# Attention and two mixtures of experts on one core: two cleared tiles of the router, and where job 14 puts a sum

## The chip, the core and the metric

The kernel runs on one core of a Trainium2 chip. The metric is the device time of one execution in microseconds, as the median of three runs. One execution is profiled, and all rows below are of that one.

## What is computed

Three layers follow each other. The first is attention over 2 batches x 8 heads, where each pair of queries is averaged. Its output becomes 1152 rows of 512. The second layer (called moe1 here) runs every row through 4 experts and adds the results with weights. The third (moe2) sends every row to the one expert of 8 with the highest score.

```python
q_pool = q.reshape(B, H, S // 2, 2, D).mean(axis=3)          # B,H,S,D = 2,8,1152,64
scores = scale * q_pool @ k.transpose(0, 1, 3, 2)
attn = exp(scores - max); attn /= attn.sum(-1) + 1e-9
x = (attn @ v) as [1152, 512]
for e in range(4):  out += p[:, e] * (relu(x @ w1[e]) @ w2[e])
x = out
logits = normalised(x) @ normalised(expert_emb).T / tau       # 8 experts
idx = argmax(logits); gate = softmax(logits)[idx]
for e in range(8):  out[idx == e] = gate * (relu(x[idx == e] @ w1[e]) @ w2[e])
```

## The kernel before

**Attention** is cut into 16 jobs (`g` = 0 to 15). A job is a pair of heads and one part of their queries: 256 columns in an even job, 320 in an odd one. `streams` multiplies keys by queries for nine chunks of 128 keys (L120, into PSUM tiles `S`, two for each of the two heads), and ACT takes the exponential of each into a tile `E` (L123, ten of them). POOL adds the nine `E` of a job into `es` (L148; the tile is shown as `y` in odd jobs). `av` multiplies the `E` by v on PE (L154), two products for each chunk. `total(g)` multiplies `es` by ones on PE (L157), which gives the denominators, and ACT copies them out as `r` (L159). `norm` has three steps: ACT copies the products out of PSUM as `x` (L163), DVE takes the reciprocal of `r` in two halves (L165), and DVE multiplies `x` by it (L167). `normalise(g)` is `total` and the last two steps. `fin` splits the normalised `x` into a high part (ACT, L174) and a low part (POOL, for job 15 DVE, L175), which the first layer of moe1 reads.

The jobs overlap: the sum and the normalising of job 13 stand inside job 14, in the middle of its products with v (L228), those of job 14 stand behind the products of job 15 (L245), and those of job 15 (`end`, L247) stand in moe1 between the first and the second layer of its first batch.

**moe1** takes the rows in three batches of 384 for each of four experts. In the first layer, eight groups of twelve matmuls (L301 to L303) fill one of three PSUM tiles `ps` each; ACT and DVE read a group out as `hh` (L305) and `hl` (L306), after which its tile can be filled again. Weights come by DMA and are split into a high and a low part by ACT (L262) and DVE (L265). The second layer (L316 to L318) follows.

**The router** (`router`, L406) prepares moe2. `block(t)` runs once for each 128 rows when moe1 has finished them, at about 572 us for the first; `place`, `table` and `finish` make the lists of rows. Two of its tiles are cleared by a memset on DVE: the first row of `base` (how many rows each expert has had so far, L416) and the last three columns of `ear` (L494). Both tiles are in a pool that is opened after attention's pools have been closed, so they lie in memory that attention used.

The program's text is not the order of the work. Where `manual_schedule` is on, the order is that of the text for attention, and for moe1's first expert on PE, ACT and DVE; elsewhere a scheduler places each instruction as early as it finds. It put both memsets, which need no input, in the middle of attention's end.

Of the kernel before, what the change touches and what calls it, by code (L numbers as in the profile page):

```python
# [9 lines left out]
def attention(tc, q, k, v, xT, identF, cc, rp, emb, tau, prep, begin, second, keep, NJ=16):  # L10
# [7 lines left out]
    with ExitStack() as ctx:  # L18
# [13 lines left out]
        def load(p):  # L32
            b,h0=divmod(2*p,H)
            kn=ld.tile([128,NC,2,D],F32,name="kn"); qn=ld.tile([128,2,5,2,D],F32,name="qn"); vn=vp.tile([128,2,NC,D],F32,name="vn")
            st['ld',p]=kn,qn; st['v',p]=vn
            ek,eq=(nc.sync,nc.scalar) if p==0 else (nc.sync,nc.sync)
            ks=[slice(0,3),slice(3,6),slice(6,9)] if p==0 else [slice(0,9)]
            for n in range(2):
                eq.dma_start(qn[:,n,0:4],q[b,h0+n,0:1024].rearrange("(i p r) d -> p i r d",p=128,r=2))
                eq.dma_start(qn[:,n,4],q[b,h0+n,896:1152].rearrange("(p r) d -> p r d",r=2))  # L40
            for c in ks:
                for n in range(2): ek.dma_start(kn[:,c,n],k[b,h0+n].rearrange("(p c) d -> p c d",c=NC)[:,c])
            if p>1: load_v(p)
        def load_v(p):
            b,h0=divmod(2*p,H)
            for n in range(2): (nc.scalar if p==0 else nc.sync).dma_start(st['v',p][:,n],v[b,h0+n].rearrange("(p c) d -> p c d",c=NC))
        def qsum(p):
            qn=st['ld',p][1]
            qs=kq.tile([128,5,2,D],F32,name="qs",bufs=1); st['qs',p]=qs
            qv=qn.rearrange("p h i r d -> p i h r d")  # L50
            for n in range(2): (nc.gpsimd if p else nc.vector).tensor_tensor(out=qs[:,:,n],in0=qv[:,:,n,0],in1=qv[:,:,n,1],op=ALU.add)
# [41 lines left out]
        def smax(g,i,early=False):  # L93
            for h in range(2): smax1(g,i,h,early)
# [5 lines left out]
        def neg(g):  # L100

            u=g%2; m=st.pop(('m3',g)); M=MM[u]
            nc.vector.tensor_reduce(out=M[:,0:2,:,0],in_=m[:,0:2],axis=AX.X,op=ALU.max,negate=True)
            if u: nc.vector.tensor_reduce(out=M[:,2,:,0],in_=m[:,2,0:1].to_broadcast([128,2,3]),axis=AX.X,op=ALU.max,negate=True)
# [44 lines left out]
        def av(g,c0,c1):  # L149
            p,u=divmod(g,2); n=JOB[u][1]; vn=st['v',p]  # L150
            if c0==0: st['O',g]=psO.tile([128,320],F32,name="O"); st['x',g]=keep['x'] if g==NG-1 else fp.tile([128,320],F32,name="x")
            O=st['O',g]
            for c in range(c0,c1):
                for h in range(2): nc.tensor.matmul(O[HD[h],0:n],vn[:,h,c],st['E',g,c][:,h,0:n],start=c==0,stop=c==NC-1)  # L154
# [5 lines left out]
        def norm(g,n0):  # L160
            n=JOB[g%2][1]; r=st.get(('r',g)); x=st['x',g]
            if n0==0:
                nc.scalar.copy(x[:,0:n],st['O',g][:,0:n])  # L163
            if n0==1:
                for a in range(0,n,n//2): nc.vector.reciprocal(r[:,a:a+n//2],r[:,a:a+n//2])  # L165
            if n0==2:
                nc.vector.tensor_tensor(out=x[:,0:n],in0=x[:,0:n],in1=r[:,0:n],op=ALU.mult)  # L167
# [10 lines left out]
        def E1(): return ep.tile([128,2,320],F32,name="E").rearrange("p h n -> p (h n)")  # L178
        route_emb_load(nc,cc,E1(),one.tile([128,1],F32,name="tb"),emb,tau)
        with tc.manual_schedule():  # L180
            qsum(0)
            load(1)
            kT(0,0); kT(0,1); st['low',0](); qT(0)
            smax(0,0,True); smax(0,1,True); st['low',1]()
            kT(0,2); st['low',2]()
            norms,scale,turn=route_emb(tc,cc,rp,E1(),one.tile([128,5],F32,name="n2"),identF)
            norms()
            for i in range(2,6): smax(0,i,True)
            scale()
            load_v(0)  # L190
            neg(0); mT(0)
            load_v(1)
            def normalise(g): total(g); norm(g,1); norm(g,2)
            for g in range(NG):
                p,u=divmod(g,2); last=g==NG-1

                rl=[(j,i) for j,i in [(g+1,i) for i in (3,4,5)]+[(g+2,i) for i in (0,1,2)] if j<NG]
                if g==0: qsum(1)
                elif u==0 and p+2<NP: load(p+2)
                elif g==NG-4: begin()  # L200
                elif u and p+2<NP: qsum(p+2)
                def between(c,hh,i):
                    if hh==1 and i==3 and c==2 and last: fin(g-2)
                def whole():

                    if not last: mT(g+1)
                    if u==0 and p+1<NP:
                        for c in range(3): tmax(p+1,c,S1(c,384) if c<2 else None)
                    if u and p+2<NP:
                        for n in range(3): kT(p+2,n,S1(n,384) if n<2 else None)  # L210
                        qT(p+2)
                if g==0:
                    streams(0,range(C1),[(1,i) for i in range(6)],PAT[3],between)
                    for c in range(3): tmax(0,c)
                    turn(T1(32).rearrange("p (d e) -> p d e",e=8))
                    for n in range(3): kT(1,n)
                    neg(1); qT(1)
                    load(2)
                    streams(0,range(C1,NC),rl[3:],PAT[2],between)
                    whole()  # L220
                    av(0,0,NC); norm(0,0)
                elif (1, 1)[u]:
                    streams(g,range(NC),rl,PAT[0],between)
                    whole()
                    if g>1 and not last: fin(g-2)
                    if g==NG-2: prep[0][2]()
                    if not last:
                        av(g,0,2); normalise(g-1)  # L228
                        if g==NG-3:
                            for i in range(3): prep[i][1]()  # L230
                        if g==NG-2: prep[3][1](); prep[1][2]()
                        av(g,2,NC); norm(g,0)
                else:
                    streams(g,range(C1),rl[:3],PAT[1],between)
                    if g>1 and not last: fin(g-2)
                    if not last:
                        normalise(g-1); av(g,0,3)
                    streams(g,range(C1,NC),rl[3:],PAT[2],between)
                    if not last:
                        whole()  # L240
                        av(g,3,NC); norm(g,0)
            g=NG-1
            prep[2][2](); prep[3][2]()
            kqx.close(); second()
            av(g,0,NC); normalise(g-1); norm(g,0); fin(g-1)  # L245
# [160 lines left out]
def router(tc, c, rp, keep, psX, y, ysc, al, identF):  # L406
    nc=tc.nc
    V=nc.vector
# [4 lines left out]
    oh=P('oh',[NT,8],BF16); gate=P('gate',[NT]); base=P('base',[NT+1,8]); R=P('R',[NT])  # L413
    ro=P('ro',[NT]); gp=P('gp',[NT,3],BF16)
    ear=P('ear',[NT]); q=P('q',[NT]); Bm=P('Bm',[NT,128],BF16)
    V.memset(base[:,0],0.0)  # L416
    es=P('es',[2,8]); ei=K('ei',[2],I32)
    cap=P('cap',[8]); sv=P('sv',[8])
    res={'ei':ei}
    def block(t):  # L420
        def S(name,shape): return rp.tile([128]+shape,F32,name="r_"+name,bufs=2)
        ts=slice(t,t+1)
# [14 lines left out]
        rk=psX.tile([128,2,8],F32,name="lr")  # L437
        nc.tensor.matmul(rk[:,1],c['ones'],oh[:,t],start=True,stop=True)
        nc.tensor.matmul(rk[:,0],c['low'],oh[:,t],start=True,stop=True)
        V.tensor_tensor(out=base[:,t+1],in0=base[:,t],in1=rk[:,1],op=ALU.add)  # L440
        rank=S('rank',[8]); V.tensor_tensor(out=rank,in0=rk[:,0],in1=base[:,t],op=ALU.add)
        w=S('w',[8]); V.tensor_tensor(out=w,in0=oh[:,t],in1=rank,op=ALU.mult)
# [41 lines left out]
    def place(a,b):  # L484

        n=b-a; ts=slice(a,b)
        ls=look(f'ls{a}',sv,a,b)
        if a==0:
            lc=look(f'lc{a}',cap,a,b)
            V.tensor_tensor(out=ear[:,ts],in0=R[:,ts],in1=lc,op=ALU.is_lt)  # L490
            ne=P('ne',[n]); V.tensor_scalar(out=ne,in0=ear[:,ts],scalar1=-1.0,scalar2=1.0,op0=ALU.mult,op1=ALU.add)
            l0=ls; ls=P('l0',[n]); V.tensor_tensor(out=ls,in0=l0,in1=ne,op=ALU.mult)
        else:
            V.memset(ear[:,ts],0.0)  # L494
        r2=P(f'r2{a}',[n]); V.tensor_tensor(out=r2,in0=R[:,ts],in1=ls,op=ALU.subtract)
        qm=P(f'qm{a}',[n,9]); V.tensor_tensor(out=qm,in0=bc(r2[:,:,None],[n,9]),in1=bc(c['thr'][:,None,1:10],[n,9]),op=ALU.is_ge)
        V.tensor_reduce(out=q[:,ts],in_=qm,axis=AX.X,op=ALU.add)
        V.scalar_tensor_tensor(out=ro[:,ts],in0=q[:,ts],scalar=-128.0,in1=r2,op0=ALU.mult,op1=ALU.add)

        g=gate[:,ts]  # L500
        V.tensor_copy(gp[:,ts,0],g)
        g1=P(f'g1{a}',[n]); V.tensor_tensor(out=g1,in0=g,in1=gp[:,ts,0],op=ALU.subtract)
        V.tensor_copy(gp[:,ts,1],g1)
        V.tensor_tensor(out=gp[:,ts,2],in0=g1,in1=gp[:,ts,1],op=ALU.subtract)
# [366 lines left out]
```

## Time and profile before

| | |
|---|---|
| median of three runs | 798.37 us (797.63 to 798.45) |
| the profiled execution | 798.72 us, of which the span from first to last instruction is 797.0 us |
| PE (TensorE matmul) busy | 769.5 us, 97% of the span |
| DVE, ACT, POOL busy | 387.0, 316.5 and 252.5 us |
| mean granted clock of TensorE | 0.993 |

Every engine works through its own queue in order; an instruction at its head that waits holds all that stand behind it. In the rows, an idle time stands in brackets behind the instruction that ended it, with what released it; "issue" means that the profile shows no releaser. Durations of successive matmuls overlap, so the step from start to start is what one costs.

### The profile page before, as it was taken

To read this page: it belongs to the slowest core of one execution; us is meant where nothing else is said; L and a number is where in the kernel's file an instruction comes from. 1 tells how busy PE (TensorE), PEld (TensorE's weight loads), DVE (VectorE), ACT (ScalarE), POOL (GpSimd) and SP (SyncE) were. 2 spreads that over 40 slices of the span, in tenths; PEclk is the share of its full clock that TensorE was granted. 3 is DMA by queue.
4 is the path that set the end of the run, shared out by engine and by line. 5 is a ranking of instruction groups with operands and counts; after the bars stand their busy time and mean duration, and the time that the engine had idled before them with its cause. 6 is when DMAs were issued, how large, how long until landed. Compare 5 with 4: busy or idle time off the path is not lost. (4 is left out here: it accounts for less than half of the span.)

```text
span 797.0 us, 13133 instructions
## 1 busy us (share of the span) xinstructions
PE 769.5 (97%) x5112; PEld 648.9 (81%) x5112; DVE 387.0 (49%) x815; ACT 316.5 (40%) x722; POOL 252.5 (32%) x224
## 2 busy tenths in 40 slices
PE   5999999999997999999999999999999999999996
PEld 3787878787767898998989989899898889877773
DVE  4778888888764220251214412144252568574520
ACT  3477667676871121250103301033131354474611
POOL 4489999999996000000000000000000201231001
PEclk9999999999998999999999999999999999999999
DMA  8412332140043100150003100000044141888992
GB/s 225 116 49 46 94 94 66 30 164 2 6 128 137 49 1 1 30 208 0 1 1 107 53 1 1 1 1 0 27 146 185 51 162 31 313 281 312 329 354 89
DMA packets 57735, 77.52 MB, mean 97 GB/s; under 512 B 23031, under 2 KB 33271, under 8 KB 57664
## 3 DMA queue, kind: packets, MB, share of 16 engines
q1 hardware_dynamic: 54272, 70.35, 26.7%
q0 software_dynamic: 1600, 4.98, 1.8%
q10 hardware_dynamic: 1792, 1.26, 0.6%
q8 instruction: 42, 0.69, 0.4%
q14 instruction: 29, 0.24, 0.1%
HBM read 71.86 MB, written 4.98 MB: 96 GB/s over the span
## 5 line engine op out<-in xcount | busy, mean ns | idle before, releaser
L301 PE MATMUL ps<-xb,w 128*128 128x384 f32 x384 | 130.6, 340 | 5.2 <-DVE hl L306 5.2
L303 PE MATMUL ps<-xb,w 128*128 128x384 f32 x384 | 130.3, 339 | 0.0
L447 POOL TENSOR_TENSOR r_n<-r_ss,half 128x1 f32<-128x1 f32 x9 | 5.3, 587 | 392.1 <-ACT X L446 392.1
L305 ACT ACTIVATE hh<-ps 128x384 fp32r<-128x384 f32 x96 | 47.1, 492 | 203.0 <-PE ps L303 203.0
L306 DVE SCALAR_TENSOR_TENSOR hl<-ps,hh 128x384 fp32r<-128x384 f32 x96 | 53.4, 556 | 148.6 <-ACT hh L305 148.4
L318 PE MATMUL py<-w,hl 128*128 128x512 f32 x288 | 113.5, 394 | 0.0
L317 PE MATMUL py<-w,hh 128*128 128x512 f32 x288 | 113.2, 393 | 0.0
L316 PE MATMUL py<-w,hh 128*128 128x512 f32 x288 | 112.8, 392 | 0.0
L123 ACT ACTIVATE E<-S 128x320 f32<-128x320 f32 (+1 forms) x288 | 98.7, 411 | 18.0 <-PE S L120 11.1
L90 DVE TENSOR_REDUCE m<-T 128x1 f32<-128x384 f32 x180 | 89.9, 549 | 18.1 <-PE T L89 16.6
L302 PE MATMUL ps<-xc,w 128*128 128x384 f32 x288 | 97.6, 339 | 0.0
L265 DVE TENSOR_TENSOR w<-st,w 128x1024 fp32r<-128x1024 f32 x60 | 76.0, 1290 | 39.2 <-ACT w L262 38.4
L148 POOL TENSOR_TENSOR y<-y,E 128x640 f32<-128x640 f32 x56 | 89.9, 1605 | 4.3
L120 PE MATMUL S<-qh,kh 64*128 64x320 f32 (+1 forms) x288 | 85.9, 342 | 0.0
L120 PE MATMUL S<-qh,kl 64*128 64x320 f32 (+1 forms) x288 | 80.2, 305 | 0.0
L148 POOL TENSOR_TENSOR es<-es,E 128x512 f32<-128x512 f32 x56 | 75.4, 1347 | 11.5 <-ACT E L123 7.4
L120 PE MATMUL S<-ql,kh 64*128 64x320 f32 (+1 forms) x288 | 78.0, 303 | 0.0
L301 PEld LDWEIGHTS ps<-xb,w 128*128 128x128 f32 x384 | 72.9, 190 | 6.3 <-DVE hl L306 5.5
L120 PE MATMUL S<-mr,ones 64*128 64x320 f32 (+1 forms) x288 | 76.3, 295 | 0.0
L154 PE MATMUL O<-E,vn 128*64 128x320 f32 (+1 forms) x576 | 75.7, 408 | 0.0
L262 ACT CAST w<-st 128x1024 fp32r<-128x1024 f32 x60 | 60.9, 1050 | 33.5 <-PE py L318 22.7
L303 PEld LDWEIGHTS ps<-xb,w 128*128 128x128 f32 x384 | 72.8, 190 | 0.0
(377 smaller groups left out, 1470.1 us busy)
## 6 DMA issues: line engine op xcount, KB each, us to landing
st<-in_moe_w SPq DMA_DIRECT2D x104, 512.0 KB, 6.2
kn<-in_k SPq DMA_DIRECT2D x14, 288.0 KB, 4.8
vn<-in_v SPq DMA_DIRECT2D x14, 288.0 KB, 3.3
qn<-in_q SPq DMA_DIRECT2D x14, 256.0 KB, 4.2
ysc<-y SPq DMA_DIRECT2D x9, 256.0 KB, 2.1
qn<-in_q SPq DMA_DIRECT2D x14, 64.0 KB, 3.5
kn<-in_k SPq DMA_DIRECT2D x6, 96.0 KB, 4.0
vn<-in_v ACTq DMA_DIRECT2D x2, 288.0 KB, 6.1
```

What stands on the lines that cost most here:

```text
L90: nc.vector.tensor_reduce(out=m[:,t,h,c:c+1],in_=s,axis=AX.X,op=ALU.max)
L120: nc.tensor.matmul(s,l[hd],r[hd],start=i==0,stop=i==3)
L123: nc.scalar.activation(out=st['E',g,c][:,h,0:n],in_=s,func=AF.Exp)
L148: nc.gpsimd.tensor_tensor(out=s,in0=st['E',g,0][:,:,0:n] if c==1 else s,in1=st['E',g,c][:,:,0:n],op=ALU.add)
L154: for h in range(2): nc.tensor.matmul(O[HD[h],0:n],vn[:,h,c],st['E',g,c][:,h,0:n],start=c==0,stop=c==NC-1)
L265: def low(): (nc.vector if le=='V' else nc.gpsimd).tensor_tensor(out=wl,in0=st,in1=wh.bitcast(F32),op=ALU.subtract)
L301: nc.tensor.matmul(ps,wh[:,fs],xh[dc],start=(dc==0),stop=False)
L302: nc.tensor.matmul(ps,wh[:,fs],xl[dc],start=False,stop=False)
L303: nc.tensor.matmul(ps,wl[:,fs],xh[dc],start=False,stop=(dc==3))
L316: nc.tensor.matmul(py,hh[:,us],wh[:,cs],start=(fc==0),stop=False)
L317: nc.tensor.matmul(py,hh[:,us],wl[:,cs],start=False,stop=False)
L318: nc.tensor.matmul(py,hl[:,us],wh[:,cs],start=False,stop=(fc==7))
```

## The change

It has two parts. The two memsets are replaced by multiplications by zero, which have to wait for their input: `base` takes its zeros from the first count of rows in block 0, `ear` from the ranks `R` of the last three blocks. And in job 14 alone (`g==NG-2`), all 18 products with v (a matmul for each half of a pair) come first, then the sum of job 13; before, 4 stood ahead of it and 14 behind.

```diff
@@ attention @@
                     if not last:
-                        av(g,0,2); normalise(g-1)
+                        c=NC if g==NG-2 else 2
+                        av(g,0,c); normalise(g-1)
                         if g==NG-3:
                             for i in range(3): prep[i][1]()
                         if g==NG-2: prep[3][1](); prep[1][2]()
-                        av(g,2,NC); norm(g,0)
+                        av(g,c,NC); norm(g,0)
@@ router @@
-    V.memset(base[:,0],0.0)
@@ block @@
         nc.tensor.matmul(rk[:,0],c['low'],oh[:,t],start=True,stop=True)
+        if t==0: V.tensor_scalar(out=base[:,0],in0=rk[:,1],scalar1=0.0,scalar2=None,op0=ALU.mult)
         V.tensor_tensor(out=base[:,t+1],in0=base[:,t],in1=rk[:,1],op=ALU.add)
@@ place @@
-            V.memset(ear[:,ts],0.0)
+            V.tensor_scalar(out=ear[:,ts],in0=R[:,ts],scalar1=0.0,scalar2=None,op0=ALU.mult)
```

What that does to the order of the instructions is seen at three places. In the new kernel the line numbers of code that follows an added line are higher by one or two. The first place is DVE at the end of attention: the last splits of weights, the normalising of job 14 (256 columns), and the first read-outs of moe1. Before:

```order
L265 TENSOR_TENSOR w<-st,w 128x1024 [waits DMAHW1_49,Activation_49]
L265 TENSOR_TENSOR w<-st,w 128x1024 [waits DMAHW2_49,PE_49,Activation_49]
L265 TENSOR_TENSOR w<-st,w 128x1024 [waits DMAHW4_49,PE_49,Activation_49]
L416 MEMSET base 128x8 [waits DMAHW5_49,PE_49]
L494 MEMSET ear 128x3 [waits Pool_49]
L165 RECIPROCAL r<-r 128x128 [waits Activation_49]
L165 RECIPROCAL r<-r 128x128
L167 TENSOR_TENSOR x<-x,r 128x256 [waits DVE_49]
L306 SCALAR_TENSOR_TENSOR hl<-ps,hh 128x384 [waits Activation_49] x2
L265 TENSOR_TENSOR w<-st,w 128x1024 [waits DMAHW5_49]
```

The same place now:

```order
L266 TENSOR_TENSOR w<-st,w 128x1024 [waits DMAHW1_49,Activation_49]
L266 TENSOR_TENSOR w<-st,w 128x1024 [waits DMAHW2_49,PE_49,Activation_49]
L266 TENSOR_TENSOR w<-st,w 128x1024 [waits DMAHW4_49,PE_49,Activation_49]
L165 RECIPROCAL r<-r 128x128 [waits Activation_49]
L165 RECIPROCAL r<-r 128x128
L167 TENSOR_TENSOR x<-x,r 128x256 [waits DVE_49,Pool_49]
L307 SCALAR_TENSOR_TENSOR hl<-ps,hh 128x384 [waits DMAHW5_49,Activation_49] x2
L266 TENSOR_TENSOR w<-st,w 128x1024 [waits DMAHW5_49]
L307 SCALAR_TENSOR_TENSOR hl<-ps,hh 128x384 [waits Activation_49] x2
```

The memsets are gone from here, with their waits for PE, a DMA queue and POOL; the multiplication of `x` has got a wait for POOL of its own, and the read-outs one for the DMA queue. The second place is PE in job 14, around the sum of job 13 (`y_106` by `y_107`), as a difference:

```order
 L120 MATMUL S_3687<-mr_3514,ones 128x256
 L109 MATMUL T<-identF,MM_147 128x128 x3
-L154 MATMUL O<-E,vn 64x256 x4
+L154 MATMUL O<-E,vn 64x256 x18
 L157 MATMUL T<-y_106,y_107 64x320 x2
-L154 MATMUL O<-E,vn 64x256 x14
 L120 MATMUL S_3743<-qh,kh 128x320
 L120 MATMUL S_3745<-qh,kh 128x320
```

All products of job 14 stand ahead of the sum now, and the scores of job 15 directly behind it. The third place is PE in moe2, where the router's last table (`dAm`, which DVE makes) is multiplied, nine times in a row, of which one stands here. Before:

```order
L615 MATMUL ps<-xb_7414,xc_6876 128x512
L613 MATMUL ps<-w,xc_6876 128x512
L614 MATMUL ps<-w,xc_6876 128x512
L615 MATMUL ps<-w,xc_6876 128x512
L516 LDWEIGHTS Bm
L516 MATMUL X<-dAm,Bm 128x30
```

And now:

```order
L615 MATMUL ps<-xb_7414,xc_6876 128x512
L616 MATMUL ps<-xb_7414,xc_6876 128x512
L614 MATMUL ps<-w,xc_6876 128x512
L615 MATMUL ps<-w,xc_6876 128x512
L517 LDWEIGHTS Bm
L517 MATMUL X<-dAm,Bm 128x30
```

The table's products stand one matmul earlier: the last of the layer (L616 now) follows behind them. The queues of ACT, POOL and SP have the same instructions in the same order as before.

## Rows read from the trace of the kernel before

**Rows 1.** Waits of PE: what waited, for whom, us in total, times, longest.

```profile
PE ps L301 <- DVE hl L306: 5.2, 1, 5.2
```

**Rows 2.** Timeline of PE, start of moe1: start us, us, instruction.

```profile
242.93 0.34 PE L303 MATMUL ps<-xb,w 128*128 128x384 f32 x1
248.48 0.69 PE L301 MATMUL ps<-xb,w 128*128 128x384 f32 x1 [5.21 <-DVE hl L306]
...
260.67 0.34 PE L302 MATMUL ps<-xc,w 128*128 128x384 f32 x1
...
261.38 0.34 PE L303 MATMUL ps<-xb,w 128*128 128x384 f32 x1
261.65 0.76 PE L157 MATMUL X<-y,y 128*64 128x320 f32 x4
```

**Rows 3.** Timeline of DVE, 244 to 250 us.

```profile
244.50 0.94 DVE L165 RECIPROCAL r<-r 128x128 f32<-128x128 f32 x1 [7.13 <-issue]
244.52 0.06 DVE L494 MEMSET ear<- 128x3 f32 x1
...
246.29 1.67 DVE L167 TENSOR_TENSOR x<-x,r 128x256 f32<-128x256 f32 x1
247.88 0.54 DVE L306 SCALAR_TENSOR_TENSOR hl<-ps,hh 128x384 fp32r<-128x384 f32 x1
...
249.39 1.22 DVE L265 TENSOR_TENSOR w<-st,w 128x1024 fp32r<-128x1024 f32 x1
```

**Rows 4.** Timeline of POOL, 244 to 252 us: adds of job 15.

```profile
244.53 3.14 POOL L148 TENSOR_TENSOR y<-y,E 128x640 f32<-128x640 f32 x2
...
249.45 2.56 POOL L148 TENSOR_TENSOR y<-y,E 128x640 f32<-128x640 f32 x1
```

**Rows 5.** Timeline of ACT, 237 to 248 us.

```profile
237.56 0.49 ACT L159 ACTIVATE r<-T,y 128x256 f32<-128x256 f32 x1
...
247.99 0.50 ACT L174 CAST xb<-x 128x192 fp32r<-128x192 f32 x2 [8.35 <-DVE x L167]
```

**Rows 6.** Stretches: us; busy time of PE, PEld, DVE, ACT, POOL; PEclk; DMA; GB/s.

```profile
243.00:248.00 5.00, 0.27 (x2) 0.00 (x0) 3.47 (x5) 0.01 (x1) 4.76 (x4) 0.90 0.00 0
248.00:254.00 6.00, 5.52 (x18) 5.52 (x19) 3.34 (x6) 1.75 (x5) 4.77 (x4) 0.52 0.17 36
```

**Rows 7.** Timeline of DVE behind block 0 of the router.

```profile
578.82 0.75 DVE L324 SCALAR_TENSOR_TENSOR y<-py,p,y 128x512 f32<-128x512 f32 x1 [2.94 <-PE py L318]
```

**Rows 8.** Timeline of PE in job 14.

```profile
218.05 1.08 PE L154 MATMUL O<-E,vn 128*64 128x256 f32 x8
220.21 0.76 PE L157 MATMUL T<-y,y 128*64 128x320 f32 x4 [1.07 <-POOL y L148]
220.80 3.19 PE L154 MATMUL O<-E,vn 128*64 128x256 f32 x28
223.92 0.41 PE L120 MATMUL S<-qh,kh 64*128 64x320 f32 x2
```

**Rows 9.** Timeline of ACT, 221 to 227 us.

```profile
221.01 0.53 ACT L159 ACTIVATE r<-T,y 128x320 f32<-128x320 f32 x1 [0.67 <-PE T L157]
...
224.12 0.37 ACT L163 COPY x<-O 128x256 f32<-128x256 f32 x1 [1.64 <-PE O L154]
224.80 1.43 ACT L123 ACTIVATE E<-S 128x320 f32<-128x320 f32 x4 [0.31 <-PE S L120]
...
227.08 0.46 ACT L174 CAST xb<-x 128x320 fp32r<-128x320 f32 x1
```

**Rows 10.** Timeline of DVE, 221 to 225 us.

```profile
221.57 2.16 DVE L165 RECIPROCAL r<-r 128x160 f32<-128x160 f32 x2 [4.45 <-ACT r L159]
223.84 1.45 DVE L167 TENSOR_TENSOR x<-x,r 128x320 f32<-128x320 f32 x1
```

**Rows 11.** Timelines of DVE and PE at the router's last table in moe2.

```profile
678.86 0.29 DVE L511 TENSOR_TENSOR dAm<-A,i 128x135 bf16<-128x135 f32 x1
...
679.16 0.40 PE L615 MATMUL ps<-w,xc 128*128 128x512 f32 x1
```

## The prediction

> **What bounds the kernel now.** PE is busy for 97% of the span (the table above), so only what keeps PE waiting, or slows it, can be won. I read PE's waits first. The longest single one that does not lie at the very start is 5.2 us, at a first-layer matmul that waits for DVE's read-out `hl` [rows 1]. PE's timeline shows where: three groups of moe1's first batch have filled the three PSUM tiles, the last matmul starts at 242.93, and the next one comes at 248.48 [rows 2]. The reader then goes to DVE at that time: for the 7.13 us before 244.50 it did nothing, which the profile calls "issue", and then the reciprocals of job 14, the multiplication L167 and the first `hl` ran one behind the other, without a gap [rows 3]. One instruction sits at the end of that idle time, the memset of `ear`, at 244.52. In DVE's queue it stands ahead of the reciprocals and it waits for POOL; that the record of L165 starts 0.02 us before it only says that both came at once. What it waited for is in POOL's timeline: one of the adds of job 15 ends and the next starts at 244.53 [rows 4]. `ear` lies in memory that attention used, and by these times the memset waited until an `E` tile there had been added. The reciprocals' own input was long there: ACT's L159 started at 237.56 and took 0.49 [rows 5].
>
> PE pays a second time. The granted clock was 0.90 in the stretch of the pause and 0.52 from 248 to 254, while PE was at work again [rows 6]; that is nearly all time at 1.2 GHz instead of 2.4.
>
> **The change, part by part.**
>
> *The memset of `ear` leaves DVE's queue.* The reciprocals can start when L159 ends, 237.56 + 0.49 = 238.05. From the first reciprocal to `hl` it took 247.88 - 244.50 = 3.38, and `hl` itself 0.54 [rows 3]: 238.05 + 3.38 + 0.54 = 241.97. PE asks for that tile one matmul step behind 242.93. The step is (261.38 - 260.67) / 4 = 0.1775 [rows 2], so at 243.11: `hl` is 1.1 us ahead, and the pause goes, 248.48 - 243.11 = **5.37 us**. On ACT the two high parts of job 14 (L174, 0.50) stand ahead of the second `hh`; they came 0.11 behind the start of the first `hl` [rows 3, 5], so now at 241.54, and end at 242.04. The second and third read-outs follow within a microsecond each, and PE needs each tile only twelve steps, 2.1 us, after the one before.
>
> *The clock.* From 248.48 to the last matmul of the fifth group from there, 261.38, are 59 steps, 12.90 us. Without a pause I see no reason for the clock to fall, since PE had no gap before. At 0.1775 they take 10.47: **2.43 us**. The low end of a step is 0.17 (matmuls overlap their neighbours by half of 0.34), which gives 2.87.
>
> So PE comes to the sum of job 15 (L157, 261.65, 0.27 behind that matmul) at 243.11 + 10.47 + 0.27 = 253.85. The next thing that could be late there is POOL. Its last add ended at 249.45 + 2.56 = 252.01, and was long because a split of weights (L265, 1.22) ran beside it on DVE; the others took 3.14 / 2 = 1.57 [rows 3, 4]. DVE's second split, two read-outs further down its queue, came behind the adds; it now falls among them and costs another 2.56 - 1.57 = 0.99, so the adds end at 253.00, 0.85 before PE asks. I cost this at nothing; the cover is those 0.85. The Trainium skill (page "SBUF — State Buffer", section "SBUF: two separate sides") goes further: a VectorE instruction with two SBUF inputs and a GpSimd one lock a shared pair of ports for their whole length, and the other one blocks. By that, L167, which has two such inputs, would hold up an add as a split does. The trace agrees for the split, and not for L167: the add beside it (the second of the two from 244.53) shows no more than 1.57. With the rule in full the time is that of the first rival.
>
> *The memset of `base`* ran without a wait of its own behind the splits, and DVE was idle after it; its removal is worth nothing. The multiplications by zero that replace both are one short DVE instruction each. In block 0 DVE has 2.94 us of idle time behind it before the next work [rows 7]: nothing.
>
> *Job 14.* PE waited 1.07 for POOL in front of the sum of job 13. (Each product shows as two matmuls, so 8 and 28 of them.) Their step is (223.92 - 220.80) / 28 = 0.111 [rows 8]; all 36 take 4.01, so the sum comes at 222.06, when POOL has long finished, and with its 220.80 - 220.21 = 0.59 the scores of job 15 start at 222.65 instead of 223.92. That is 1.27 earlier, but ACT is not: the sum's read-out L159 comes 0.80 behind the sum [rows 8, 9], so at 222.86 instead of 221.01. From L159 to the first exponential ACT took 224.80 - 221.01 = 3.79, of which 1.64 and 0.31 were waiting, so 1.84 of work: first exponential at 224.70, 0.1 earlier than before. PE has two score tiles for each head, so from the third chunk on it waits for these exponentials. Behind the sixth stands L174 for job 13, at 227.08 [rows 9], which needs L167. L165 came 0.56 behind the start of L159, L167 2.27 behind that, and took 1.45 [rows 9, 10]: 222.86 + 0.56 + 2.27 + 1.45 = 227.14, just late. The exponentials behind it, and PE, end 0.1 later than before. I take **0.1 lost**: the 1.07 come back as short waits for score tiles. The ends are 1.07 won, if ACT keeps up, and 0.5 lost, if L167 takes 1.67 as at 246.29 and the read-out of the sum is late too.
>
> *The router's last table.* Its products stand one matmul earlier, so PE comes to them at 679.16, where the last matmul of the layer stood. DVE finishes the table at 678.86 + 0.29 = 679.15 [rows 11], now later by the zeroing of `ear` ahead of it, for which the memset's 0.06 [rows 3] is the nearest row. I take **0.1 lost**, between 0 and 0.2.
>
> **Sum**, against the profiled execution: 798.72 - 5.37 - 2.43 + 0.1 + 0.1 = 791.1. The median of the runs is 0.35 below that execution, so I predict **790.8 us**. Everything behind moe1's first batch hangs on PE, whose other waits there are short, so it moves as a whole. With the ends of the terms (0.44 more from the clock, 1.17 and 0.1 less lost; or 0.4 and 0.1 more lost), this case alone reaches from 789.1 to 791.3.
>
> **Rivals.**
>
> *POOL is the next bound.* If L167 holds up an add for its 1.67, the adds end at 253.00 + 1.67 = 254.67, 0.8 us after PE asks: 791.6. If in turn a split on DVE stands behind two adds, 2 x 1.57, the later read-outs come 3.1 late, of which the 1.1 that `hl` is ahead covers a part: 2 more, 793.6. For it: POOL has no gap in this time. Against it: the add beside L167. A pause as short as job 14's 1.07 left the step behind it at 0.111, as fast as any, so I charge no slow clock for it.
>
> *The idle time was not the memset's.* If L165 itself was held until 244.50 by something that the trace does not name, the pause stays, and the time is 798.4 with the two terms of 0.1: 798.6. For it: the row puts the idle time in front of L165, as "issue". Against it: its only wait is for ACT, and the same pair for job 13 ran right behind its L159 [rows 9, 10].
>
> *The wait comes back, later.* L167 has got a wait for POOL of its own, and the order does not say for which of POOL's instructions. In earlier jobs the same wait guards `x` against the low part made from the same buffer three jobs before, long done by then. But should it be for the last add, then L167 runs at 252.01 instead of 246.29, and everything behind comes 5.72 later, with the pause and the slow clock kept: 798.4 + 5.7 = 804.1. It decides at 246.29: a POOL instruction that ends later makes the kernel slower than it was. Against it: L167 of job 13 carries such a wait, and started at 223.84, when its reciprocals were done (221.57 + 2.16), while POOL was in the middle of its adds.
>
> **How the numbers follow.** The forecast gets 0.78, the first rival 0.12, the second 0.06, the third 0.04. The range is to hold 8 in 10: from 789.0, the low end of the forecast, to 793.5, which takes in most of the first rival. A measurement of this kernel can tell 0.2%, 1.6 us, from no change. Forecast and first rival are both faster by more: 0.90. The second is no change: 0.06. The third is slower: 0.04.
>
> **What would show it.** In the new profile, DVE's first reciprocal of job 14 starts near 238.1 and the first `hl` near 241.4; PE's wait of 5.2 for `hl` is gone; the granted clock is 1.00 from 243 to 254; the sum of job 15 stands near 253.9, and POOL's last add ends near 253.0. In job 14 there is no wait for POOL at L157, and yet the products of job 15 start at about the same time as before. It would be wrong if DVE is idle again ahead of L165 or L167, if PE waits at L157 in moe1, or if PE's later waits grow by what was won here.

## The result, and the profile after

The median is **791.37 us** (789.44 to 792.29, six runs) beside 798.41 (797.56 to 801.77, six runs) for the kernel before on the same chip: over all runs a ratio of 0.9904 (the quotient of the two medians would be 0.9912), 95% interval 0.9883 to 0.9925. The profiled execution took 790.55 us, its span is 788.8 us, the mean granted clock 0.997.

PE's waits first. The 5.2 for `hl` [rows 1] is gone, and one of 0.8 is new, for an exponential:

```profile
PE T L58 <- DMA kn<-in_k: 6.6, 2, 5.2
...
PE S L120 <- ACT E L123: 0.8, 1, 0.8
```

PE's timeline at the start of moe1. The fourth group, which stood still for 5.21 [rows 2], starts a matmul's step behind the third, at 242.25, and the sum of job 15 follows the first layer at once:

```profile
235.79 0.44 PE L302 MATMUL ps<-xb,w 128*128 128x384 f32 x1
...
242.08 0.34 PE L304 MATMUL ps<-xb,w 128*128 128x384 f32 x1
242.25 0.34 PE L302 MATMUL ps<-xb,w 128*128 128x384 f32 x1
...
252.68 0.34 PE L304 MATMUL ps<-xb,w 128*128 128x384 f32 x1
252.94 0.76 PE L157 MATMUL X<-y,y 128*64 128x320 f32 x4
```

DVE at that time. The reciprocals start 0.13 behind the last split of weights (233.44 + 3.08 = 236.52), where [rows 3] had 7.13 of idle time, and the first `hl` ends at 240.66, 1.6 before PE asks for its tile. The last line is L167 of job 15, which runs when POOL is idle:

```profile
233.44 3.08 DVE L266 TENSOR_TENSOR w<-st,w 128x1024 fp32r<-128x1024 f32 x2 [0.68 <-ACT w L263]
236.65 1.76 DVE L165 RECIPROCAL r<-r 128x128 f32<-128x128 f32 x2
...
238.52 1.67 DVE L167 TENSOR_TENSOR x<-x,r 128x256 f32<-128x256 f32 x1
240.11 0.55 DVE L307 SCALAR_TENSOR_TENSOR hl<-ps,hh 128x384 fp32r<-128x384 f32 x1
...
241.62 1.92 DVE L266 TENSOR_TENSOR w<-st,w 128x1024 fp32r<-128x1024 f32 x1
...
256.51 0.49 DVE L167 TENSOR_TENSOR y<-y,r 128x320 f32<-128x320 f32 x1
```

POOL's adds of job 15 [rows 4]. Two are now long, one for each split of weights, and the last ends at 250.88 + 1.58 = 252.46, 0.48 before PE's L157:

```profile
238.33 1.57 POOL L148 TENSOR_TENSOR y<-y,E 128x640 f32<-128x640 f32 x1
239.87 1.06 POOL L175 TENSOR_TENSOR xc<-x,xb 128x320 fp32r<-128x320 f32 x1
240.90 1.57 POOL L148 TENSOR_TENSOR y<-y,E 128x640 f32<-128x640 f32 x1
...
242.54 2.44 POOL L148 TENSOR_TENSOR y<-y,E 128x640 f32<-128x640 f32 x1
...
250.88 1.58 POOL L148 TENSOR_TENSOR y<-y,E 128x640 f32<-128x640 f32 x1
```

The stretches of [rows 6], in which PEclk was 0.90 and 0.52:

```profile
243.00:248.00 5.00, 5.00 (x30) 5.00 (x29) 3.92 (x5) 0.98 (x2) 4.84 (x3) 1.00 0.00 0
248.00:254.00 6.00, 6.00 (x35) 5.21 (x34) 1.73 (x4) 1.72 (x4) 5.14 (x5) 1.00 0.09 16
```

PE in job 14 and at the start of job 15 [rows 8]: no wait at L157, then the new one at the third chunk's scores:

```profile
217.39 4.11 PE L154 MATMUL O<-E,vn 128*64 128x256 f32 x36
221.32 0.71 PE L157 MATMUL T<-y,y 128*64 128x320 f32 x4
221.96 0.41 PE L120 MATMUL S<-qh,kh 64*128 64x320 f32 x2
...
224.20 0.74 PE L120 MATMUL S<-qh,kh 64*128 64x320 f32 x2 [0.80 <-ACT E L123]
...
230.36 5.07 PE L154 MATMUL O<-E,vn 128*64 128x320 f32 x36
```

ACT there [rows 9]: it now stands idle for 2.32 in front of the later sum, and its cast L263, 1.04, comes behind that:

```profile
222.08 0.53 ACT L159 ACTIVATE r<-T,y 128x320 f32<-128x320 f32 x1 [2.32 <-PE T L157]
222.50 1.04 ACT L263 CAST w<-st 128x1024 fp32r<-128x1024 f32 x1
...
226.12 0.46 ACT L174 CAST xb<-x 128x320 fp32r<-128x320 f32 x1
```

POOL and DVE there: L167 of job 13, for which L174 waits, takes 1.18, where [rows 10] had 1.45; an add has started ahead of it:

```profile
224.45 1.28 POOL L148 TENSOR_TENSOR es<-es,E 128x512 f32<-128x512 f32 x1
...
224.91 1.18 DVE L167 TENSOR_TENSOR x<-x,r 128x320 f32<-128x320 f32 x1
```

The last table in moe2 [rows 11]: DVE has finished it 0.12 before PE starts on it, and PE's step there is 0.24, as between any two:

```profile
670.12 0.29 DVE L512 TENSOR_TENSOR dAm<-A,i 128x135 bf16<-128x135 f32 x1
670.29 0.40 PE L615 MATMUL ps<-w,xc 128*128 128x512 f32 x1
...
670.53 0.39 PE L517 MATMUL X<-dAm,Bm 128*128 128x30 bf16 x9
```

**Where the time came from.** From the first product of job 14 to L157 of job 15, PE took 261.65 - 218.05 = 43.60 before and 252.94 - 217.39 = 35.55 now: 8.05 of the 8.17 between the two profiled executions. What lies outside of this stretch moves by itself: in the 13 executions profiled here the first product of job 14 stands between 216.06 and 219.66, and the part behind L157 takes between 533.2 and 538.6; the last section shows a part of what moves it. So the experiments below are read by this stretch first, and by the median second.

### The profile page after: what moved, and what is told of

The parts are those of the page before. It is cut to its first block, busy times and chain, and to the rows that moved or that the text cites. A ratio compares the mean times of both kernels' runs of the same rounds, so it can differ in the third digit from the quotient of the medians.

```text
span 788.8 us, 13134 instructions
## 1 busy us (share of the span) xinstructions
PE 766.4 (97%) x5112; PEld 646.2 (82%) x5112; DVE 389.4 (49%) x815; ACT 316.2 (40%) x722; POOL 253.6 (32%) x224
## 5 line engine op out<-in xcount | busy, mean ns | idle before, releaser
L266 DVE TENSOR_TENSOR w<-st,w 128x1024 fp32r<-128x1024 f32 x60 | 78.3, 1329 | 38.7 <-ACT w L263 37.9
L263 ACT CAST w<-st 128x1024 fp32r<-128x1024 f32 x60 | 60.9, 1049 | 35.2 <-PE py L319 22.7
```

What stands on the lines that cost most here:

```text
L266: def low(): (nc.vector if le=='V' else nc.gpsimd).tensor_tensor(out=wl,in0=st,in1=wh.bitcast(F32),op=ALU.subtract)
```

## The experiments

My theory: the memset of `ear` held DVE's queue, because `ear` lies where an `E` tile of job 15 lay; from that come the pause and the slow clock. The order of job 14 moves a wait and is worth a few tenths at most. The rivals: the new order of job 14 has a part in it, `base` has one, or it is the memset as an instruction and not its memory.

| kernel | median us | ratio, 95% interval | us from job 14's first product to the sum of job 13 (L157), to the products of job 15, to moe1 | us from moe1's start to L157 | pause us |
|---|---|---|---|---|---|
| before | 798.37 | 1 | 2.16, 13.28, 18.71 | 24.89 | 5.21 |
| the change | 791.37 | 0.9904 (0.9883 to 0.9925) | 3.93, 12.97, 18.40 | 17.15 | none |
| zeros alone | 790.92 | 0.9906 (0.9890 to 0.9921) | 2.26, 13.37, 18.80 | 16.84 | none |
| job 14 alone | 799.32 | 1.0019 (0.9997 to 1.0040) | 3.94, 12.96, 18.39 | 25.00 | 5.50 |
| `base` alone | 798.70 | 1.0004 (0.9990 to 1.0018) | 2.20, 13.32, 18.75 | 25.14 | 5.19 |
| `ear` elsewhere | 790.21 | 0.9893 (0.9859 to 0.9927) | 2.17, 13.30, 18.73 | 16.84 | none |

Each ratio, here and below, is over all runs, and against the kernel before as run on the same chip, where its median was between 798.38 and 799.22. So rows are compared by their ratios and not by their medians.

**The zeros alone.** The change, with job 14 in its old order:

```diff
-                        c=NC if g==NG-2 else 2
+                        c=2
```

> The two multiplications by zero alone, job 14 in its old order. My theory: the memset of ear held DVE, so all of the pause (5.4) and of the slow clock (2.4) go here as in the full change; PE waits about 1.1 for POOL at L157 of job 14 again, and the products of job 15 come about 0.3 later than in the full change. Time 0.991 of before, about 0.3 above the full change: 791.7. Rival (the new order of job 14 is what lets DVE start early): the idle time ahead of L165 and PE's wait of 5.2 stay, 798.

All of the gain that the medians can tell is here. L157 of job 14 waits 1.17 for POOL again, and the products of job 15 come 13.37 behind the first of job 14 instead of 12.97. Moe1's first layer was 0.31 quicker in this execution, so that the whole stretch takes 35.64 beside 35.55; the last section shows that such a difference also comes between kernels that are the same up to there. On DVE the reciprocals wait for ACT's L159 and for nothing else; the first line is POOL's add beside them:

```profile
237.24 1.57 POOL L148 TENSOR_TENSOR y<-y,E 128x640 f32<-128x640 f32 x1
...
236.43 1.76 DVE L165 RECIPROCAL r<-r 128x128 f32<-128x128 f32 x2 [0.72 <-ACT r L159]
...
238.30 0.80 DVE L167 TENSOR_TENSOR x<-x,r 128x256 f32<-128x256 f32 x1
239.02 0.55 DVE L307 SCALAR_TENSOR_TENSOR hl<-ps,hh 128x384 fp32r<-128x384 f32 x1
```

**Job 14 alone.** The kernel before, with `c=NC if g==NG-2 else 2` and nothing else.

> The new order of job 14 alone, both memsets kept. My theory: no wait for POOL at L157 of job 14, PE reaches moe1 about 0.3 earlier, but the memset is released by POOL, whose adds do not come earlier by as much, so that the pause grows by what was won: 798.1 to 798.4, no change that can be measured. Rivals: the 0.3 or the whole 1.07 is kept (797.3), or this order removes the pause (791).

PE comes to moe1 0.32 earlier, and its pause is 0.29 longer. DVE's release comes from POOL, at its own time:

```profile
246.19 0.94 DVE L165 RECIPROCAL r<-r 128x128 f32<-128x128 f32 x1 [7.40 <-issue]
246.21 0.06 DVE L495 MEMSET ear<- 128x3 f32 x1
```

A gain ahead of a wait that somebody else ends is a longer wait. The interval allows 0.03% faster at best, so neither 797.3 nor 791 is left.

**`base` alone.** The kernel before, with the memset of `base` replaced as in the change and that of `ear` kept.

> Only the memset of base replaced, that of ear kept, job 14 in its old order. My theory: base held nothing; the idle time of DVE ahead of L165, PE's wait of 5.2 and the stretch at half clock all stay: 798.4, ratio 1.000 within 0.002. Rival: the waits that base's memset carried (a DMA queue and PE) were part of what held DVE; then some or all of the 7.8 goes, 791 to 797.

Nothing changes: a pause of 5.19, and 7.14 of DVE's idle time ends with the memset of `ear`:

```profile
242.53 0.94 DVE L165 RECIPROCAL r<-r 128x128 f32<-128x128 f32 x1 [7.14 <-issue]
242.56 0.06 DVE L494 MEMSET ear<- 128x3 f32 x1
```

**`ear` in other memory.** Both memsets stay memsets, and job 14 keeps its old order:

```diff
-    ear=P('ear',[NT]); q=P('q',[NT]); Bm=P('Bm',[NT,128],BF16)
+    ear=K('ear',[NT]); q=P('q',[NT]); Bm=P('Bm',[NT,128],BF16)
```

> The kernel before, with both memsets and job 14 in its old order; only the tile ear lies in a pool that is opened ahead of attention, in memory that attention does not use. My theory: its memset held DVE because of the E tile that lay in the same memory; here it waits for nothing, so the pause and the slow clock go as with the zeros taken from data: moe1's start to L157 16.8 to 17.2, 791. Rival (a memset of DVE, or its place in the queue, is what costs): the pause stays, 798.

This is as good as taking the zeros from data (35.57). With memory of its own the memset waits for nothing, and the scheduler put it at the start of the program; that of `base`, which still lies in attention's old memory, stays in the queue and costs nothing, since its wait is over by then:

```profile
0.98 0.06 DVE L494 MEMSET ear<- 128x3 f32 x1
...
238.65 0.07 DVE L416 MEMSET base<- 128x8 f32 x1
239.42 1.76 DVE L165 RECIPROCAL r<-r 128x128 f32<-128x128 f32 x2 [0.71 <-ACT r L159]
```

So the cause is the reuse of the memory: it tied a memset of moe2's router to an add of attention. This run changed the memset's place in the queue together with its wait; the runs that follow put a memset with a wait back at the old place, and tell the two apart.

### What a pause costs

The kernel of the change, with a wait put back: ahead of L165 of job 14 a memset of three columns in an `E` tile of job 15 whose add is POOL's second, third or fifth (chunk 2, 3 or 5). Nothing reads these columns afterwards.

```diff
-            av(g,0,NC); normalise(g-1); norm(g,0); fin(g-1)
+            av(g,0,NC); total(g-1); nc.vector.memset(st['E',g,2][:,0,0:3],0.0); norm(g-1,1); norm(g-1,2); norm(g,0); fin(g-1)
```

> The full change, with one short DVE memset put back ahead of L165 of job 14. It writes three columns of an E tile of job 15 (the third chunk's, which is needed no more behind its add), so it waits for POOL's second add of job 15. By the profile of the changed kernel that add ends 4.1 behind the start of moe1 on PE; from L165 to the end of the first hl DVE takes 4.0, so the fourth group, which PE reaches 6.5 behind the start of moe1, comes at 8.1: a pause of 1.6. Theory A (the slow clock is a fixed price of any pause): 1.6 and 2.4 lost, moe1's start to L157 21.2 instead of 17.15, 795.4. Theory B (the price grows with the pause, 2.4 for 5.4): 1.6 and 0.7, 19.5, 793.7. Theory C (a pause this short costs itself alone): 1.6, 18.8, 793.0, and the granted clock stays 1.00. Rival to all: such a memset does not hold the reciprocals, no pause, 17.15, 791.4.

> The same, with the memset in the fourth chunk's E tile: it waits for POOL's third add of job 15, which ends 6.7 behind the start of moe1. First hl at 10.7, a pause of 4.2. Theory A: 4.2 and 2.4 lost, moe1's start to L157 23.8, 798.0. Theory B: 4.2 and 1.9, 23.2, 797.5. Theory C with a limit above 4.2: 21.3, 795.6. Rival: no pause, 791.4.

> The same, with the memset in the sixth chunk's E tile: it waits for POOL's fifth add, which, without a split beside it, ends about 9.9 behind the start of moe1. First hl at 13.9, a pause of 7.4, longer than the one of the kernel before. Theory A: 7.4 and 2.4 lost, moe1's start to L157 27.0, 801.2. Theory B: 7.4 and 3.3, 27.9, 802.1. Rival: no pause, 791.4.

The medians are 791.72 (0.9911, 0.9888 to 0.9934), 797.26 (0.9978, 0.9965 to 0.9991) and 799.76 (1.0022, 1.0006 to 1.0038). With one tiny memset the gain is lost again where the add that it waits for is late (chunks 3 and 5), and almost all of it is kept where the add is early (chunk 2), so it is the wait that costs and not the memset or its place. The pauses were 0.77, 3.96 and 7.09, each shorter than expected; at chunk 2 L167 took 0.82, and not the 1.67 that was counted. Of the theories of the clock, A fails at chunk 2, where the clock did not fall, and B at chunk 5, which lost less to the clock than chunk 3; C holds at chunk 2, but not as far as chunk 3. Two more runs filled the gap between 0.77 and 3.96, with two or four memsets of 640 columns behind the small one:

```diff
+            for _ in range(2): nc.vector.memset(st['E',g,1],0.0)
```

> The run with the short wait (a pause of 0.77 with the clock at 1.00), and behind its memset two more of 640 columns in an E tile that is needed no more: a pause of 1.5 to 3. If the clock falls after every pause that is longer than about one us, a stretch of half clock of 6.8 as in the three runs that had one, from about 3.4 to 4.4 behind PE's last matmul: most of it with PE at work, so about 3 lost beside the pause. If a pause must outlast those 3.4 us for that: no half clock, only the pause lost.

> The same with four more memsets: a pause of 2.2 to 4.3. Same two theories: half clock for 6.8, about 3 lost beside the pause; or, where the pause stays under 3.4, none.

Each ran once, in 799.37 and 798.90 us. Of the 8.8 and 8.4 by which that is above the profiled execution of the change, 4.0 and 4.4 lie between job 14's first product and L157; the rest lies ahead of it and behind it, so these two are read by the stretch alone. Neither theory held: with pauses of 2.29 and 2.76 the clock was at half for 3.4, and not for 6.8 or not at all. In the run with two of them, where the reciprocals don't start together with the small memset, the profile names outright what it waited for:

```profile
242.09 0.06 DVE L246 MEMSET E<- 128x3 f32 x1 [3.46 <-POOL y L148]
```

PE's first matmul behind the pause, in four of these runs (chunk 2; chunk 2 with two more memsets; chunk 3; chunk 5):

```profile
245.05 0.44 PE L302 MATMUL ps<-xb,w 128*128 128x384 f32 x1 [0.77 <-DVE hl L307]
```

```profile
246.82 0.44 PE L304 MATMUL ps<-xb,w 128*128 128x384 f32 x1 [2.29 <-DVE hl L309]
```

```profile
246.88 0.69 PE L302 MATMUL ps<-xb,w 128*128 128x384 f32 x1 [3.96 <-DVE hl L307]
```

```profile
248.96 0.69 PE L302 MATMUL ps<-xb,w 128*128 128x384 f32 x1 [7.09 <-DVE hl L307]
```

The granted clock comes from stretches of 2 us. Here are those of chunk 5; a stretch at 0.94 has 2 x 0.06 / 0.5 = 0.24 us at 1.2 GHz, one at 0.85 has 0.6, and three lie at 0.50 throughout: 6.8 in all, of which PE works from 248.96 to 252.6.

```profile
244.00:246.00 2.00, 0.00 (x0) 0.00 (x0) 1.02 (x3) 0.00 (x0) 1.92 (x2) 0.94 0.00 0
246.00:248.00 2.00, 0.00 (x0) 0.00 (x0) 1.97 (x2) 0.00 (x0) 1.92 (x2) 0.50 0.00 0
248.00:250.00 2.00, 1.04 (x3) 1.04 (x4) 1.52 (x4) 1.27 (x4) 1.92 (x3) 0.50 0.00 0
250.00:252.00 2.00, 2.00 (x7) 2.00 (x7) 1.96 (x2) 0.00 (x0) 1.67 (x2) 0.50 0.52 137
252.00:254.00 2.00, 2.00 (x11) 2.00 (x11) 0.47 (x1) 0.49 (x1) 0.00 (x0) 0.85 1.00 395
```

The same for all, with what was lost beside the pause (moe1's start to L157, less 17.15 and the pause; the 17.15 is itself uncertain by 0.3, as the last section shows):

| pause | at 1.2 GHz in all | of it with PE at work | lost beside the pause |
|---|---|---|---|
| 0.77 (chunk 2) | 0 | 0 | 0.2 |
| 2.29 (two more memsets) | 3.4 | 3.4 | 1.7 |
| 2.76 (four more memsets) | 3.4 | 3.4 | 1.7 |
| 3.96 (chunk 3) | 6.8 | 6.2 | 2.9 |
| 5.21 (the kernel before) | 6.8 | 5.3 | 2.5 |
| 7.09 (chunk 5) | 6.8 | 3.6 | 1.8 |

What a pause costs beside itself is about half the time that PE then works at 1.2 GHz. A pause of 7.09 therefore lost less to the clock than one of 3.96, since 3.2 of its 6.8 at 1.2 GHz fell into the pause, and 0.6 of chunk 3's. Two runs from above fit too: `base` alone, with a pause of 5.19, had 6.1 of slow work and lost 2.8; job 14 alone, with a longer pause of 5.50, had 4.9 and lost 2.4. With four memsets one `hl` ran ahead of L167, so that row has a slightly other order on DVE; its pause and clock are read like the others.

### What the order of job 14 is worth

**The cast earlier.** The change, with ACT's cast L263 moved ahead of the sum, into the 2.32 that ACT is idle:

```diff
-                    if g==NG-2: prep[0][2]()
+                    if g==NG-2: prep[0][2](); prep[3][1]()
...
-                        if g==NG-2: prep[3][1](); prep[1][2]()
+                        if g==NG-2: prep[1][2]()
```

> The full change, with ACT's last cast of a weight in job 14 (L263, 1.04) moved ahead of the sum of job 13, into the 2.32 that ACT is idle there. My theory of job 14 is that ACT, behind the later sum, sets when the exponentials of job 15 come: the first comes about 1.0 earlier, PE's new wait of 0.8 for it goes, and the products of job 15 start 0.5 to 0.8 earlier. PE then asks at L157 of job 15 at about 252.2 where POOL's adds end at 252.46 or a little earlier: between 0.3 and 0.8 faster than the full change, 790.6 to 791.1. Rival: the exponentials are not what bounds the products (L174 or POOL is): the wait moves to another place and the time stays at 791.4.

A miss: 791.79 (0.9923, 0.9908 to 0.9939), and the stretch takes 35.53 beside 35.55. The first exponential does come earlier, but PE's wait, 0.79 here, only moved two chunks on. ACT shows why: L174, the high part of job 13, stands among the exponentials and waits for L167 of DVE. In the change L167 ended at 226.09 and the exponential ahead of L174 at 226.10, so both held L174 equally, and making only one of them earlier could win next to nothing.

```profile
224.79 0.46 ACT L174 CAST xb<-x 128x320 fp32r<-128x320 f32 x1 [0.84 <-DVE x L167]
```

**The high part later, too.** L174 of job 13 two chunks further down ACT's queue:

```diff
-                    if hh==1 and i==3 and c==2 and last: fin(g-2)
+                    if hh==1 and i==3 and c==4 and last: fin(g-2)
```

> The early cast as before, and in ACT's queue in job 15 the high part of job 13 (L174, which needs L167 of DVE) stands behind the exponentials of the fifth chunk instead of those of the third. My theory, after the last runs: L174 with its wait for L167 is what holds the exponentials, and PE's 0.8 with them. Then the 0.8 goes, the products of job 15 start 12.1 to 12.3 behind those of job 14 (12.94 with the early cast alone), and at L157 PE meets POOL, whose last add ended 35.03 behind: L157 at 35.0 to 35.1 instead of 35.53. Rival (ACT's own work, or POOL, holds the exponentials): products still at 12.9, L157 at 35.5. The total differs by too little to be told: 790.5 to 791.5 in either case.

PE's wait is gone, and the products of job 15 start 11.98 behind those of job 14, 0.96 earlier. Only 0.26 of that arrives, because PE now meets POOL's last add. L157 comes at 35.27 and not at the 35.0 to 35.1 expected, as that add ended later too, at about 35.2 instead of 35.03:

```profile
254.91 0.76 PE L157 MATMUL X<-y,y 128*64 128x320 f32 x4 [0.63 <-POOL y L148]
```

The median is 790.58 (0.9885, 0.9855 to 0.9914). By the trace it is the shortest of the stretches, by 0.26; the medians can't tell it from the change.

## Why the prediction was right, and where it was not

- **Result.** 790.8 forecast, 791.37 measured, inside 789.0 to 793.5 and faster by more than 0.2%.
- **The pause and the clock (5.37 + 2.43 = 7.80).** From moe1's start to L157 24.89 became 17.15, 7.74 less. The mechanism is shown by parts: the zeros alone bring it, `ear` in other memory brings it too, and a memset that waits for an add takes it away again. The clock's price was right for this pause: pauses of 5.19 and 5.50 lost 2.8 and 2.4 beside themselves, and other lengths between 0.2 and 2.9.
- **`hl` 1.1 ahead.** It is 1.6 ahead: the first reciprocal started 0.86 behind moe1's start and not 1.29. POOL's last add ends 0.48 before PE asks, not 0.85: a second long add was added as foreseen, but, counted from job 14's first product, PE came 0.25 earlier than forecast (without the 0.1 that job 14 was to lose) and the add 0.12 later.
- **Job 14 (0.1 lost).** The mechanism was right: most of the 1.07 came back as a wait of 0.80 for an exponential, and what holds the products of job 15 is L174 behind L167, as the last two runs show. The term was mis-sized. L167 took 1.18 (224.91 to 226.09) and not the 1.45 of [rows 10], and L159 came 0.12 earlier than forecast, so the products of job 15 came 0.31 earlier (13.28 to 12.97; 0.40 beside the zeros alone). That is too little for the medians, and where the memset stays it only makes the pause longer.
- **The table (0.1 lost).** Nothing was lost; DVE was 0.12 early. The zero for `base` took 0.17 in block 0, where 2.73 of idle time remain [rows 7].
- **The median, 0.35 below the profiled execution.** This step carried nothing. In 23 later runs the kernel before spread from 795.0 to 802.0, so one execution against a median of three says little about a third of a microsecond.
- **The rivals.** That the idle time was not the memset's fell with the first run, and so did a later wait: L167 ran right behind its reciprocals. POOL as the next bound was the right next bound: it did not show in the change, 0.48 away, and showed as a wait of 0.63 as soon as PE was made 0.96 earlier.
- **A wrong reading, without a price here by luck.** I wrote that the trace speaks against a lock between L167 and an add, because the add beside it was no longer than 1.57. The add had started first, and it was L167 that waited. In the change the add from 238.33 ends at 239.90 and L167 at 240.19; with the zeros alone, an add of POOL from 237.24, 1.57 long, ends at 238.81 and L167 at 239.10. In both L167 ends 0.29 behind the add, whenever it started, and so 1.67 is long and 0.80 short. L167 of job 13, with 320 columns, ends 0.35 behind the add that had started ahead of it, in the kernel before and in the change; that add ended at 224.94 and at 225.74, and this alone made 1.45 into 1.18. Behind attention, with POOL idle, L167 of 320 columns takes 0.49. The other way round, the add of 2.44 from 242.54 ended 1.44 behind the split that ran from 241.62 to 243.54, and so had to wait for it. The Trainium skill (page "SBUF — State Buffer", section "SBUF: two separate sides") states just this: the instruction that starts first has the shared pair of ports for its whole length, and the other one blocks. The trace agrees, in both directions. In all 13 executions an add had started before L167 of job 13 and of job 14, so DVE paid and the add did not; had L167 come first, the first rival's price could have been due.

## What to carry to other kernels

A tiny instruction without inputs is not free to place: if its tile reuses memory, it waits for the last reader there, and in an in-order queue all behind it wait too. Give such tiles memory of their own, or make their clearing late by giving it a late input; each took 1% off the time here. Before a wait is removed on one engine, ask who ends the next one: what was gained ahead of POOL's release came back as a longer pause. And where two-input work of VectorE and adds of GpSimd run side by side, read both durations, because the one that started second shows the wait.

## What was not expected of the hardware

- The price of a pause in clock is not fixed and does not simply grow with the pause: beside the pause itself, 0.2 was lost at 0.77, where the clock did not fall, 1.7 at 2.29 and 2.76, 2.9 at 3.96, 1.8 at 7.09. The stretch at 1.2 GHz was 3.4 us behind pauses of 2.29 and 2.76, and 6.8 behind each of those from 3.96 on. After 2.29, the clock fell only when PE had been at work again for 1.2 us.
- The step of the same matmuls in moe1's first layer has two values at a granted clock of 1.00: 0.1733 with the zeros alone and with `ear` elsewhere, 0.1767 in the change. It does not go by the kernel's text alone: the runs with chunk 2 and with chunk 5 are the same up to their memset, and PE's first three groups had steps of 0.1733 and 0.1767. But all four executions with job 14 in its old order had 0.1733 there, and of the nine with the new order seven had 0.1767, chunk 3 0.175 and chunk 2 0.1733, so a part of the new order is not ruled out. Over 96 matmuls that is 0.3 us, nearly as much as the new order won ahead of moe1. The step also changes within an execution: in the kernel before, it was 0.1733 ahead of the pause, 0.1767 when the clock was back, and 0.1734 on average between 300 and 560 us. In `base` alone and in the two runs with more memsets it was 0.1767 there too; over some 750 steps that is 2.5 us, most of what their part behind L157 (537.9 to 538.6) is longer than that of most others (534.6 to 536.1). No comparison of single executions here can see through such differences; why they come is open.
